# Output-weight rows loaded four to a partition, and input-weight columns read with a step of four

## The chip, the cores and the metric

The kernel runs on one core of one Trainium2 chip. The metric is the device time in microseconds (us). Of the program before there are three timed runs and one profiled execution. All kernels compute the same outputs from the same inputs.

## What is computed

A linear-attention recurrence (RWKV5) over 4 batches, 8 heads, 768 time steps and 48 channels a head feeds a two-layer perceptron with a SiLU between the layers:

```python
for t in range(S):                                   # per batch and head
    cur = outer(u * k[t], v[t])
    y[t] = r[t] @ (state + cur)
    state = w[:, None] * state + outer(k[t], v[t])
x = y as (3072 tokens, 384)
h = x @ w_in            # (384, 2048)
g = h * sigmoid(h)
out = g @ w_out         # (2048, 384)
```

All inputs and the output are 32-bit floats. Inside the kernel the perceptron's matmuls take 16-bit floats.

## The kernel before

**Units.** The 768 steps are cut into 6 chunks of 128. A unit is one chunk of one batch, so there are 24 units. Unit `i` is chunk `i // 4` of batch `i % 4`. For each unit the kernel loads r, k and v (L70), turns r and k on the tensor engine (PE, L254), applies powers of the decay (L264), forms products and sums, and evicts y in 16 bits. Then y is transposed into `xT`, the first layer's moving operand: for the first six units on PE (L465), later by a transposing transfer (L460).

**First layer.** `l1_mm` (L479) makes a piece of hidden features. `win` holds `w_in` as 128 partitions by 3 blocks `q` of 128 input features by 2048 hidden columns, in 16 bits. For hidden tile `ft` (128 of the 2048 columns, 16 tiles in all) PE loads three weight blocks, one for each `q`, and after each runs a matmul over 512 tokens (four batches) or 256 tokens (two batches, and then two tiles to a piece). `l1_silu` (L488) evicts the piece through ScalarE (ACT) into `gT`.

**Second layer.** `l2_mm` (L501) takes 128 tokens of `gT` as weights and streams `wout[:, ft, :]`, 384 columns, over the 16 tiles `ft`, four tiles to a part. `l2_last` (L525) does the same for the last unit with two column ranges.

**Weights' transfers.** `ld_win(g)` (L82) loads 512 columns of `w_in`, group `g`, and `ld_wout(g)` (L87) loads 512 rows of `w_out`, both from the queue of GpSimd (POOL), since they cast from 32 to 16 bits on the way. There are four of each.

**What sets the order.** The schedule is written by hand. Each engine runs its instructions in the order in which the program emits them. When the program is built, a wait on a semaphore is put wherever an instruction reads or overwrites a region of a tile that an earlier instruction of another engine or queue writes or reads. For the first chunk and the start of the second, the string `order` (L584) is that order, word by word; afterwards a loop over pairs of units (L617) interleaves attention steps with "fillers" from the perceptron. In the string, `L0.0` is `l1_mm` for batches 0 and 1, tiles 0 and 1; `L2.6` is batches 2 and 3, tiles 6 and 7; `L4.8` is all four batches, tile 8. A `G` word is the SiLU of the same piece. `i_q0` to `i_q3` are the four transfers of `win`, `i_o0` to `i_o3` those of `wout`. `T`, `rT`, `kT`, `kc`, `ku`, `ru`, `vu`, `S`, `Y`, `Q`, `P` are steps of a unit. `4*` in front of a word puts four matmuls of a zero tile on PE (`spin`, L163). The part that matters here reads:

```python
... 4*Y0 y160 T2 kT2 2*Y1 y161 ku2 ru2 rT2 yT0 xT0 i_q1 yT1 xT1 v162 T3 kT3 rT3 ku3 ru3 rd2
v163 4*A23 vu2 i_q2 rd3 vu3 am2 am3 L0.0 G0.0 L0.2 G0.2 Y2 y162 Y3 y163 kc0 yT2 xT2 L0.4
G0.4 kc1 yT3 xT3 L0.6 G0.6 S0 st0 kc2 T4 kT4 rT4 kc3 L2.0 G2.0 L2.2 G2.2 ku4 v164
L2.4 G2.4 S2 L2.6 G2.6 st2 ru4 i_q3 r164 L4.8 G4.8 L4.9 G4.9 rd4 ku5 kc4 kc5 sd4
L4.10 G4.10 T5 kT5 rT5 L4.11 G4.11 vu4 ru5 i_o0 v165 Q4 P4 ...
```

So three transfers of `win` are emitted ahead of `L0.0`, and the fourth between `L2.6` and `L4.8`. Hidden tiles 0 to 3 lie in group 0, tiles 4 to 7 in group 1, 8 to 11 in group 2, 12 to 15 in group 3.

Of the kernel before, what the change touches and what calls it, by code (L numbers as in the profile page):

```python
# [15 lines left out]
def kernel(  # L16
# [11 lines left out]
    nc = tc.nc  # L28
# [38 lines left out]
    win = big.tile([128, NQ, DFF], F16)  # L67
# [19 lines left out]
    def ld_wout(g):  # L87
        nc.gpsimd.dma_start(
            out=wout[:, 4 * g:4 * g + 4, :],
            in_=moe_w_out[512 * g:512 * g + 512, :].rearrange("(f p) n -> p f n", p=128))  # L90

    def columns(eng, dst, src, j):
        eng.dma_start(out=dst[64 * j:64 * j + D, :],
# [381 lines left out]
    gts = {}  # L475

    hpss = {}

    def l1_mm(sc, b0, nb, ft):  # L479
        m = B // nb  # L480
        hps = hpss[b0, ft] = ps.tile([128, m, nb * C], FP, name="hps", tag="moe", bufs=4)
        for f in range(m):
            for q in range(NQ):
                nc.tensor.matmul(hps[:, f, :], win[:, q, (ft + f) * 128:(ft + f + 1) * 128],  # L484
                                 xts[sc][:, q, b0:b0 + nb, :].rearrange("p b t -> p (b t)"),
                                 start=(q == 0), stop=(q == NQ - 1))

# [7 lines left out]
    def l1(sc, b0, nb, ft):  # L495
        l1_mm(sc, b0, nb, ft)
        l1_silu(sc, b0, nb, ft)
# [65 lines left out]
    def piece(word, f):  # L563
# [13 lines left out]
        "Y": outputs_y, "y16": evict_y, "yT": turn_y, "xT": copy_x,  # L577
        "S": first_sums, "st": first_state, "ku": bonus_ku, "ru": bonus_rku, "rd": bonus_sum,
        "r16": cast_r, "sd": decayed_state, "i_q": ld_win, "i_o": ld_wout,
        "Q": sums, "P": product_halves, "m": masked_halves, "s1_": state_first,  # L580
        "s2_": state_second, "sn": next_state, "Z": outputs_halves, "z": evict_halves,
# [14 lines left out]
    for word in order.split():  # L596
        if "*" in word:
            n, word = word.split("*")
            spin(int(n))
        if word[0] == "A":  # L600
            product_pair(int(word[1]))
        elif word in steps:
            steps[word]()
        elif word[0] == "L":
            piece(word[1:], l1_mm)
        elif word[0] == "G":
            piece(word[1:], l1_silu)
        elif word[0] == "H":
            l1(1, 0, 2, 2 * int(word[1]))
        else:  # L610
            unit_steps[word[:-1]](int(word[-1]))
# [74 lines left out]
```

## Time and profile before

| what | value |
|---|---|
| median of 3 runs (lowest to highest) | 195.09 us (194.4 to 197.38) |
| the profiled execution's own time | 194.21 us |
| its span in the profile | 192.5 us |
| PE busy | 180.4 us, 94% of the span |
| ACT, POOL, DVE (VectorE) busy | 118.5, 117.2, 107.7 us |
| first-layer matmuls (L484) | 360, the weight loads 98 ns each |
| DMA, mean over the span | 127 GB/s, about 200 GB/s in the first 45 us |
| packets of POOL's queue (q0) | 3712 packets, 3.15 MB |

The profile lists for each engine the time it was busy; "PEld" is the weight load of the tensor engine, which may run beside a matmul. A group of instructions is shown as line, engine, operation, output and input tile, shapes and count. Times in a timeline are start and length in us, counted from the start of the span; in brackets stands the idle time of the engine just before, and what ended it. A transfer's time "to landing" is counted from the start of its issue.

### The profile page before, as it was taken

To read this page: it belongs to the slowest core of one execution; us is meant where nothing else is said; L and a number is where in the kernel's file an instruction comes from. 1 tells how busy PE (TensorE), PEld (TensorE's weight loads), DVE (VectorE), ACT (ScalarE), POOL (GpSimd) and SP (SyncE) were. 2 spreads that over 40 slices of the span, in tenths; PEclk is the share of its full clock that TensorE was granted. 3 is DMA by queue.
4 is the path that set the end of the run, shared out by engine and by line. 5 is a ranking of instruction groups with operands and counts; after the bars stand their busy time and mean duration, and the time that the engine had idled before them with its cause. 6 is when DMAs were issued, how large, how long until landed. Compare 5 with 4: busy or idle time off the path is not lost. (4 is left out here: it accounts for less than half of the span.)

```text
span 192.5 us, 6544 instructions
## 1 busy us (share of the span) xinstructions
PE 180.4 (94%) x2786; PEld 112.2 (58%) x2786; DVE 107.7 (56%) x183; ACT 118.5 (62%) x235; POOL 117.2 (61%) x151
## 2 busy tenths in 40 slices
PE   7888898989999999999999999999999999899993
PEld 2455684567756876745546646557656456444562
DVE  7578775846965846836827826917924914200120
ACT  5499478779383495198593297683397773189200
POOL 6499999599899955949659459469339320000000
PEclk9999999999999999999999999999999999999999
DMA  5999999999268568278185286294286201210022
GB/s 94 215 214 198 208 200 184 159 224 217 33 117 166 184 138 169 80 149 202 29 169 136 72 178 168 46 191 125 55 166 170 41 23 66 71 52 0 2 83 83
DMA packets 90272, 24.42 MB, mean 127 GB/s; under 512 B 83329, under 2 KB 90242, under 8 KB 90242
## 3 DMA queue, kind: packets, MB, share of 16 engines
q1 hardware_dynamic: 84992, 20.39, 48.4%
q0 software_dynamic: 3712, 3.15, 10.8%
q10 hardware_dynamic: 1538, 0.46, 1.1%
q8 instruction: 22, 0.36, 0.8%
q14 instruction: 8, 0.07, 0.1%
HBM read 20.65 MB, written 4.72 MB: 132 GB/s over the span
## 5 line engine op out<-in xcount | busy, mean ns | idle before, releaser
L484 PE MATMUL hps<-xT,win 128*128 128x512 f16 (+1 forms) x360 | 66.4, 337 | 1.0 <-DMA xT<-y 0.9
L492 ACT ACTIVATE gT<-hps 128x512 f16<-128x512 f32 x96 | 55.3, 600 | 16.6 <-PE hps L484 14.1
L505 PE MATMUL ops<-wout,gT 128*128 128x384 f16 x368 | 63.0, 326 | 1.3 <-ACT gT L492 1.3
L505 PEld LDWEIGHTS <-gT 128*128 128x128 f16 x368 | 34.9, 98 | 25.4 <-ACT gT L492 2.5
L484 PEld LDWEIGHTS <-win 128*128 128x128 f16 x360 | 33.6, 98 | 26.9 <-issue 2.1
L221 POOL TENSOR_TENSOR ku<-kin,u_bc 128x384 f32<-128x384 f32 x24 | 24.7, 1029 | 15.0 <-DMA kin<-in_k_dram 11.7
L239 POOL TENSOR_TENSOR vu<-vin,rku 128x384 f32<-128x384 f32 x24 | 19.8, 837 | 19.1 <-DVE rku L234 19.1
L511 ACT COPY osb<-ops 128x384 f32<-128x384 f32 x20 | 9.6, 478 | 30.7 <-PE ops L505 27.9
L448 DVE TENSOR_TENSOR y<-yp,vu 64x384 f16<-64x384 f32 x40 | 21.3, 554 | 11.8 <-PE yp L437 5.7
L225 POOL TENSOR_TENSOR rku_f<-rin,ku 128x384 f32<-128x384 f32 x24 | 24.5, 1020 | 1.7
L392 DVE TENSOR_TENSOR s<-sp,sdec 112x384 f32<-112x384 f32 x10 | 5.6, 558 | 32.9 <-PE sp L379 30.9
L229 POOL TENSOR_TENSOR kc<-kin,lamH 128x384 f16<-128x384 f32 x20 | 20.7, 1036 | 0.0
L269 DVE TENSOR_TENSOR kT<-att,lamK 112x512 f32<-112x512 f32 x24 | 16.3, 677 | 4.7 <-PE att L261 4.7
L269 DVE TENSOR_TENSOR rT<-att,lamR 112x512 f32<-112x512 f32 x24 | 16.2, 677 | 2.3 <-PE att L261 2.3
L337 ACT CAST s1h<-s 48x384 f16<-48x384 f32 x20 | 10.2, 510 | 6.5 <-DVE s L392 6.2
L248 ACT CAST v<-vin 128x384 f16<-128x384 f32 x24 | 11.5, 510 | 2.7 <-DMA vin<-in_v_dram 2.5
L513 DVE COPY osb<-ops 128x384 f32<-128x384 f32 x3 | 1.7, 558 | 20.5 <-issue 16.4
L234 DVE TENSOR_REDUCE rku<-rku_f 128x8 f32<-128x384 f32 x24 | 12.4, 538 | 1.0 <-POOL rku_f L225 1.0
L363 DVE TENSOR_TENSOR am<-att,maskH 128x1024 f16<-128x1024 f32 x10 | 12.2, 1218 | 1.3 <-PE att L356 1.3
L283 ACT CAST rT<-rT 112x512 f16<-112x512 f32 x20 | 12.4, 620 | 0.1
L356 PE MATMUL att<-rT,kT 48*64 48x64 f32 x640 | 11.6, 220 | 0.0
L356 PEld LDWEIGHTS att<-rT,kT 48*64 48x64 f32 x640 | 10.4, 135 | 0.0
(81 smaller groups left out, 183.8 us busy)
## 6 DMA issues: line engine op xcount, KB each, us to landing
rin<-in_r_dram SPq DMA_DIRECT2D x24, 192.0 KB, 3.6
vin<-in_v_dram SPq DMA_DIRECT2D x24, 192.0 KB, 4.7
kin<-in_k_dram SPq DMA_DIRECT2D x23, 192.0 KB, 4.7
out_dram<-osb SPq DMA_DIRECT2D x23, 192.0 KB, 3.2
win<-in_moe_w_in_dram POOLq DMA_DIRECT2D x4, 384.0 KB, 6.0
wout<-in_moe_w_out_dram POOLq DMA_DIRECT2D x4, 384.0 KB, 6.4
xT<-y SPq DMA_TRANSPOSE x18, 2.3
kin<-in_k_dram ACTq DMA_DIRECT2D x1, 192.0 KB, 3.8
```

What stands on the lines that cost most here:

```text
L221: nc.gpsimd.tensor_tensor(out=L(i)["ku"], in0=kin[i % NIN][:, :, 0:D], in1=u_bc, op=ALU.mult)
L225: nc.gpsimd.tensor_tensor(out=L(i)["rku_f"], in0=rin[i % NIN][:, :, 0:D], in1=L(i)["ku"], op=ALU.mult)
L229: nc.gpsimd.tensor_tensor(out=kc[i % NIN][:, :, 0:D], in0=kin[i % NIN][:, :, 0:D], in1=lamH if unit(i)[0] else lamC, op=ALU.mult)
L234: nc.vector.tensor_reduce(out=L(i)["rku"], in_=L(i)["rku_f"], axis=mybir.AxisListType.X, op=ALU.add)
L239: nc.gpsimd.tensor_tensor(out=L(i)["vu"], in0=vin[i % NIN], in1=L(i)["rku"].unsqueeze(2).broadcast_to([128, H, D]), op=ALU.mult)
L269: nc.vector.tensor_tensor(out=L(i)[key].rearrange("p g (y t) -> p y g t", y=2), in0=L(i)["t"][0:PR, :, x], in1=lam, op=ALU.mult)
L283: nc.scalar.copy(out=L(i)["rT16"], in_=L(i)["rT"])
L356: nc.tensor.matmul(a[o0:o0 + HC, j, e, p, :], kT[r0:r0 + D, p, HC * x:HC * x + HC], rT[r0:r0 + D, p, HC * x:HC * x + HC], start=True, stop ...
L448: nc.vector.tensor_tensor(out=L(i + e)["y16"][rows].rearrange("p h d -> p (h d)"), in0=L(i)["y2"][r][rows, 0:HD], in1=L(i + e)["vu"][rows] ...
L484: nc.tensor.matmul(hps[:, f, :], win[:, q, (ft + f) * 128:(ft + f + 1) * 128], xts[sc][:, q, b0:b0 + nb, :].rearrange("p b t -> p (b t)"), ...
L492: nc.scalar.activation(out=gts[sc][:, ft:ft + m, b0 * C:(b0 + nb) * C], in_=hpss[b0, ft], func=AF.Silu)
L505: nc.tensor.matmul(opss[b], gts[sc][:, ft, b * C:(b + 1) * C], wout[:, ft, :], start=(ft == 0), stop=(ft == NFT - 1))
```

## The change

Two edits that belong together. `ld_wout` lays the 512 rows of a group out so that partition `p` holds rows `4p` to `4p + 3` of the group, instead of rows `p`, `128 + p`, `256 + p` and `384 + p`. These four rows are neighbours in memory, so a partition's part of a transfer is one run of 6144 bytes where it was four runs of 1536. The hidden feature that stands on partition `t` of tile `ft` of `wout` is now number `512 (ft // 4) + 4 t + ft % 4`. So that `gT` has the same order, the first layer's weights for tile `ft` are read from `win` as every fourth column of group `ft // 4`, from column `ft % 4` on, instead of 128 neighbouring columns. `win` is loaded as before.

```diff
     def ld_wout(g):
         nc.gpsimd.dma_start(
             out=wout[:, 4 * g:4 * g + 4, :],
-            in_=moe_w_out[512 * g:512 * g + 512, :].rearrange("(f p) n -> p f n", p=128))
+            in_=moe_w_out[512 * g:512 * g + 512, :].rearrange("(p f) n -> p f n", p=128))
...
     hpss = {}
+    win4 = win.rearrange("p q (g t c) -> p q g t c", t=128, c=4)
 
     def l1_mm(sc, b0, nb, ft):
         m = B // nb
         hps = hpss[b0, ft] = ps.tile([128, m, nb * C], FP, name="hps", tag="moe", bufs=4)
         for f in range(m):
             for q in range(NQ):
-                nc.tensor.matmul(hps[:, f, :], win[:, q, (ft + f) * 128:(ft + f + 1) * 128],
+                nc.tensor.matmul(hps[:, f, :], win4[:, q, (ft + f) // 4, :, (ft + f) % 4],
                                  xts[sc][:, q, b0:b0 + nb, :].rearrange("p b t -> p (b t)"),
                                  start=(q == 0), stop=(q == NQ - 1))
```

The order of instructions on every engine stays what it was. The waits that the build puts on them do not; on PE and POOL these differ (`<` before, `>` after; DMASW0 to DMASW3 are the four transfers of `win`, in order):

```
L0.0, 2nd weight load    < no wait                  > waits DMASW1, DMASW2
L0.4, 1st weight load    < waits DMASW1             > no wait
L4.8, 1st weight load    < waits DMASW2             > no wait
L4.8, 2nd weight load    < no wait                  > waits DMASW3
L4.12, 1st weight load   < waits DMASW3             > no wait
POOL, transfer i_q3      < no wait                  > waits PE (the last matmul of L2.6)
POOL, kc0 and kc1 (2nd)  < wait PE                  > no wait (covered by the wait above)
```

## The prediction

> **What bounds the kernel now.** The page's first part comes first: PE is busy 94% of the span. The table by stretches says where that holds.
>
> ```profile
> PE 180.4 (94%) x2786; PEld 112.2 (58%) x2786; DVE 107.7 (56%) x183; ACT 118.5 (62%) x235; POOL 117.2 (61%) x151
> ```
>
> ```profile
> 20.00:34.00 14.00, 12.21 (x222) 8.84 (x223) 9.92 (x16) 9.70 (x19) 13.88 (x16) 1.00 1.08 196
> 34.00:50.00 16.00, 14.77 (x317) 10.43 (x311) 11.30 (x19) 13.13 (x26) 13.23 (x16) 1.00 1.14 189
> 50.00:100.00 50.00, 49.92 (x827) 32.43 (x819) 32.63 (x53) 31.12 (x61) 38.52 (x45) 1.00 0.59 131
> 100.00:164.00 64.00, 62.78 (x1070) 37.67 (x1071) 36.38 (x59) 39.93 (x78) 36.27 (x41) 1.00 0.49 111
> ...
> 189.20:192.50 3.30, 0.00 (x0) 0.00 (x0) 0.00 (x0) 0.26 (x1) 0.00 (x0) 1.00 0.19 62
> ```
>
> The columns are the stretch, its length, busy time of PE, PEld, DVE, ACT, POOL, granted clock, DMA share and GB/s. PE's idle time from 20 to 164 us is 1.79 + 1.23 + 0.08 + 1.22 = 4.3 us. After 50 us PE hardly waits, so whatever PE loses early stays lost, except what those 4.3 us can give back. The chain of waits agrees: its last 25 us are PE matmuls, preceded by one transposing transfer. DMA is full up to about 48 us (share about 1), but the sorted waits from 30 to 60 us hold none of an engine for a transfer. The wout transfers, issued between 33.5 and 44 us, lie in that stretch.
>
> Then PE's timeline where the change reorders waits, and POOL's beside it:
>
> ```profile
> 19.78 1.49 PE L484 MATMUL hps<-xT,win 128*128 128x256 f16 x12
> 21.18 0.38 PE L312 MATMUL yp<-v,am 128*128 128x48 f16 x8
> 22.31 0.37 PE L312 MATMUL yp<-vx,am 128*128 128x48 f16 x8 [0.76 <-DVE am L302]
> 22.77 0.34 PE L469 MATMUL yT<-ident,y 128*128 128x128 f16 x3
> ...
> 27.92 2.77 PE L484 MATMUL hps<-xT,win 128*128 128x256 f16 x15
> ```
>
> ```profile
> 19.81 0.80 POOL L83 DMA_DIRECT2D win<-in_moe_w_in_dram  x1
> ...
> 27.28 0.80 POOL L83 DMA_DIRECT2D win<-in_moe_w_in_dram  x1
> ```
>
> The first PE row is L0.0 and L0.2, started 0.03 us before i_q2 is even issued; the last row is L2.6 (six matmuls over 256 tokens) and then L4.8 to L4.10 (nine over 512), begun after i_q3's issue. Asked for the two issues alone, the list of transfers gives 5.8 us to landing for i_q2 and 6.2 for i_q3, so they land at 25.6 and 33.5 us. Today neither is waited for.
>
> **The change part by part.**
>
> *The first new wait.* L0.0's second weight load waits for i_q2, though its columns lie in group 0. PE runs in order, so all of PE stands behind it, from about 20.0 us to 25.6. The second matmul started 0.12 us after 19.78 (12 of them take 1.49 us, the last 0.27: one in 0.11); now about 25.7. That is +5.8 us. Behind it on PE: the rest of L0.0, L0.2, Y2. ACT waits with its SiLUs, DVE with y16. POOL doesn't: its rows up to i_q3 (kc0 to kc3, ku4, ru4) need nothing of PE here.
>
> *What is given back.* Y3 waited 0.76 us for the mask product on DVE, which now is done in time; but then the transposes wait for y16 of unit 2, which DVE can only evict (0.55 us) after Y2. Replayed: Y2 ends at 27.35, y16 at 27.95, the transposes start at 28.0 against 22.77, so the shift is 5.25. The two short waits for POOL (0.21 us each, ahead of S0 and S2) go as well: 4.8 us at the end of L2.6, which now is at 28.75 (27.92, five steps of 0.11 and 0.27 for the last) and comes at 33.6.
>
> *The second new wait, a loop of two.* i_q3 now waits for L2.6's last matmul, and L4.8's second weight load waits for i_q3. L4.8 is the very next step on PE. Issue at about 33.65 instead of 27.28; landing 5.8 to 6.2 us later (its own rows; I take 6.0, the median of the four), at 39.65; the matmul starts at 39.8 instead of 28.8 (27.92, six matmuls of 0.11 and one of 0.22 us before it). The shift is 11.0 us. Queued behind i_q3 on POOL are ku5, kc4, kc5, the decayed state, vu4, ru5, i_o0: they come 6.4 us later, PE 11, so PE finds them done. SP's own transfers reuse buffers that POOL frees, by the same 6.4, less than PE's shift. The last wout transfer comes behind vu5, which waits for DVE and so for PE: it moves as PE does, and its landing (at 50.2, the part that needs it not before 52.5) keeps its place.
>
> *After that.* PE's waits for POOL go (0.42 us at 31.96), the one for ACT's cast of v (0.94) stays, since ACT casts behind the SiLU of L4.11. I take 0.6 given back: +10.4 us.
>
> *The clock.* Twice PE now stands still, 5.6 and 6.1 us. The longest idle stretch in the trace is the 3.3 us after the last matmul, at a granted clock still 1.00; so from below the cost is nothing. From above: the spins at the start.
>
> ```profile
> 2.97 1.91 PE L166 MATMUL zs<-idle 128*128 128x512 f16 x4
> ...
> 6.31 1.04 PE L166 MATMUL zs<-idle 128*128 128x512 f16 x4
> ```
>
> Four equal matmuls take 1.91 us at first and 1.04 later. The slow pace lasts from 1.29 to about 5.5 us, 4.2 us, in which work for 4.2 x 1.04/1.91 = 2.3 us gets done: 1.9 us lost. At most that after each stall, 3.8; I take half, 1.9, as the trace decides neither way. The Trainium skill, TensorE: Matmul & The Clock Gate, Part 1, speaks against the change here: it says that the array falls to half clock after one idle window of about 3.4 us and needs a busy one to come back. No row before has an idle stretch that long; by that rule, an estimate, each stall costs half of such a window, 1.7 us, and the sum would be 208.
>
> *Strided weight loads.* 360 loads read every fourth column. Each has a matmul to hide under: 109 ns (256 tokens; by the loops 144 of them) or 216 ns (512 tokens; 216 of them). Recorded are 98 ns today, and their pace where nothing hides them is
>
> ```profile
> 21.17 0.27 PEld L312 LDWEIGHTS <-am 128*128 128x128 f16 x8 [0.19 <-DVE am L302]
> ```
>
> that is (270 - 98)/7 = 25 ns. From below: nothing, a hidden load can't give time. From above: four times that pace, 100 ns, and the 37 ns by which a load of 32-bit columns (L356, 135 ns) is longer than one of 16-bit; 137 ns would show 28 ns on 144 matmuls, 4 us, and about 0.1 us on each of some 40 first loads behind a wait, 4 us: 8 us. I take 0, the 25 ns being nearer than any row with a step. The skill's TensorE: Matmul & The Clock Gate, Weight-path perf modes, lets the fast load take strided columns, and its section LDWEIGHTS gives P/1.2, 107 ns for 128 columns, without it; by either it stays hidden, and the sum is the same.
>
> *The wout transfers.* 2048 runs become 512 if each goes as one packet: q0 falls from 3712 to 2176. Issue costs 0.80 us for 384 runs (win) and 0.80 for 512 (wout), so POOL saves nothing. No wait of the trace ends with wout; between -0.5 and +0.5 us for traffic beside it, I take 0.
>
> *Sum.* 5.8 - 1.0 + 6.2 (33.65 + 6.0 + 0.15 - 28.8 - 4.8) - 0.6 = 10.4, and 1.9 for the clock: 12.3 on the profiled execution's 194.21 (span 192.5, 1.7 around it) gives 206.5. That execution is 0.9 under the median, 195.09, so the forecast is 11.4 over the median.
>
> **The rivals.**
>
> *Strides show.* The same two stalls and the 8 us: 214.5. Against it: the spare 11 to 118 ns under every matmul. It would show as matmuls of L484 spaced wider than 109 and 216 ns.
>
> *A quick i_q3.* Issued 6 us later, it may meet emptier queues: a transfer of half its size lands in a median 3.6 us. Then the second stall is 2.4 us shorter and the second clock loss falls away: 203.1. Against it: DMA moves 189 GB/s from 34 to 50 us too, as SP's transfers fill the queues.
>
> *The loss is given back (not slower).* One mechanism, PE's own slack: with other engines ahead, PE's waits vanish. Its whole idle time is 192.5 - 180.4 = 12.1 us; if all of it absorbed the two waits (12.0 without what is already given back) the time is 194 to 195. It decides from 8.1 us given back on (12.0 less 2% of 195, 3.9). Only 4.3 us lie between 20 and 164 us, so at best 194.2 + 12.0 - 4.3 = 202.
>
> *The transfers matter (faster).* DMA bounds the first 48 us and fewer packets shorten it. q0 takes 10.8% of 16 engines' span, half of it wout's; but PE's waits that end with a transfer are 0.7 + 0.9 us in all: 193 at best, and the new waits must not bind.
>
> **How the numbers follow.** Two stalls as replayed 0.68, at 206.5; strides as well 0.14, up to 214.5; a quick i_q3 0.12, at 203; given back 0.04; faster 0.02. A measurement of this kernel can tell about 2% from no change, 3.9 us. Slower by over 2%: 0.68 + 0.14 + 0.12 = 0.94; within: 0.04; faster: 0.02. The range goes from 201.5 (a quick i_q3 and no clock loss, less the rest of the slack) to 213 (3.8 us of clock, half of the strides' bound and more): it leaves out the two last cases and the upper end of the strides.
>
> **What would show it.** Right: PE idle about 5.6 us after one L484 matmul near 20 us, ended by a win transfer; i_q3 issued near 33.6, about 0.1 us after L2.6; PE idle about 6 us again, ended by it; from 50 us on the same rows 10 to 12 us later; in the granted clock a dip behind one or both stalls. L484's spacing still 109 and 216 ns. Wrong: PE at L0.2 before 25 us, a stall below 4 us, or a shift at 50 us that differs by more than 3 us from that at L4.8.

## The result, and the profile after

The changed kernel took 210.04 us (208.65 to 211.08, four runs) against 195.94 for the kernel before beside it: a ratio of 1.0743, with a 95% interval of 1.062 to 1.0867. (The ratio compares the means of the fast runs, which leave out one run of the kernel before, at 197.38 us; its median has that run.) It is slower. The profiled execution took 210.78 us, with a span of 209.1, 16.6 more than before. From the page of the changed kernel, busy times, the two rows of PE by slices and of its granted clock, POOL's DMA queue, and the first layer's groups:

```profile
PE 185.9 (89%) x2786; PEld 119.2 (57%) x2786; DVE 108.2 (52%) x183; ACT 119.0 (57%) x235; POOL 116.4 (56%) x151
...
PE   7898079078899999999999999999999999989993
...
PEclk9999859959999999999999999999999999999999
...
q0 software_dynamic: 2176, 3.15, 9.7%
...
L485 PE MATMUL hps<-xT,win 128*128 128x512 f16 (+1 forms) x360 | 69.9, 348 | 12.7 <-DMA win<-in_moe_w_in_dram 11.8
...
L485 PEld LDWEIGHTS <-win 128*128 128x128 f16 x360 | 39.1, 115 | 36.4 <-issue 9.3
```

The first-layer matmuls, whose line is now 485, waited 11.8 us for transfers of win. All of that is in two holes of PE's row, slices 5 and 8 of 40 (5.2 us each), and the clock's row dips in and behind the first (slices 5 and 6) and behind the second (slice 9). POOL's queue fell to the 2176 packets that four rows to a packet give. The timeline of PE, and below it that of POOL:

```profile
6.94 1.89 PE L166 MATMUL zs<-idle 128*128 128x512 f16 x4
...
21.05 0.30 PE L485 MATMUL hps<-xT,win 128*128 128x256 f16 x1
26.82 2.51 PE L485 MATMUL hps<-xT,win 128*128 128x256 f16 x11 [5.47 <-DMA win<-in_moe_w_in_dram]
...
35.77 1.06 PE L485 MATMUL hps<-xT,win 128*128 128x256 f16 x7
43.16 3.60 PE L485 MATMUL hps<-xT,win 128*128 128x512 f16 x8 [6.33 <-DMA win<-in_moe_w_in_dram]
...
51.05 1.49 PE L485 MATMUL hps<-xT,win 128*128 128x512 f16 x6
...
184.78 10.52 PE L485 MATMUL hps<-xT,win 128*128 128x512 f16 x48 [0.87 <-DMA xT<-y]
```

```profile
21.08 0.80 POOL L83 DMA_DIRECT2D win<-in_moe_w_in_dram  x1
...
36.91 0.80 POOL L83 DMA_DIRECT2D win<-in_moe_w_in_dram  x1 [8.35 <-PE hps L485]
...
43.11 0.61 POOL L88 DMA_DIRECT2D wout<-in_moe_w_out_dram  x1
```

One matmul of L0.0 runs; the next comes 5.8 us later, when i_q2 has landed. Six of L2.6 and one of L4.8 run; POOL, idle for 8.35 us, may now issue i_q3; 6.2 us later it has landed, and PE goes on. That is the loop: PE holds POOL, then POOL's transfer holds PE.

The shift against the kernel before, at six places of PE's timelines, says where the 16.6 us came in. Two rows of the kernel before that it rests on:

```profile
34.43 1.47 PE L484 MATMUL hps<-xT,win 128*128 128x512 f16 x6
...
168.19 10.52 PE L484 MATMUL hps<-xT,win 128*128 128x512 f16 x48 [0.87 <-DMA xT<-y]
```

| place | before | after | shift | added here |
|---|---|---|---|---|
| first matmul of L0.0 | 19.78 | 21.05 | 1.27 | 1.27 |
| its second | 19.90 | 26.82 | 6.92 | 5.65 |
| first of L2.6 | 27.92 | 35.77 | 7.85 | 0.93 |
| second of L4.8 | 28.80 | 43.16 | 14.36 | 6.51 |
| first of L4.12 | 34.43 | 51.05 | 16.62 | 2.26 |
| first of the last L484/L485 run | 168.19 | 184.78 | 16.59 | -0.03 |

After 50 us nothing is added and nothing given back. The 1.27 us at the top are no part of the change, as neither a wait nor a read differs up to there: in this execution the tensor engine ran its first matmuls at half pace for longer (the spins at 6.94 us took 1.89 us, where in the execution before the four at 6.31 took 1.04). The kernel with the step alone, below, has the same waits and starts L0.0 at 19.79. The 2.26 us are the clock, and the 0.93 the clock less some 0.6 that PE gets back; the kernel with spins, below, parts the two. The table by stretches of 2 us has it in the last column but two:

```profile
22.00:24.00 2.00, 0.00 (x0) 0.00 (x0) 1.52 (x2) 0.00 (x0) 2.00 (x3) 1.00 1.27 231
24.00:26.00 2.00, 0.00 (x0) 0.00 (x0) 0.00 (x0) 0.00 (x0) 2.00 (x3) 0.52 1.22 199
26.00:28.00 2.00, 1.18 (x6) 0.88 (x7) 0.00 (x0) 0.00 (x0) 1.92 (x3) 0.50 0.97 197
28.00:30.00 2.00, 1.97 (x23) 1.44 (x20) 0.24 (x1) 1.19 (x2) 0.57 (x1) 0.50 1.04 204
30.00:32.00 2.00, 1.63 (x16) 1.55 (x17) 0.78 (x2) 0.84 (x2) 0.00 (x0) 0.78 1.06 211
...
40.00:42.00 2.00, 0.00 (x0) 0.00 (x0) 0.00 (x0) 0.00 (x0) 2.00 (x3) 0.78 1.07 172
42.00:44.00 2.00, 0.84 (x2) 0.29 (x3) 0.00 (x0) 0.00 (x0) 1.71 (x3) 0.50 0.10 16
44.00:46.00 2.00, 2.00 (x6) 0.73 (x5) 0.00 (x0) 1.08 (x2) 0.00 (x0) 0.50 0.79 121
46.00:48.00 2.00, 2.00 (x19) 1.05 (x18) 0.16 (x1) 0.71 (x2) 0.00 (x0) 0.51 0.39 75
48.00:50.00 2.00, 1.06 (x39) 0.51 (x38) 1.13 (x2) 1.28 (x3) 0.00 (x0) 1.00 0.00 0
```

A stretch at 0.52 was at half clock for 1.92 of its 2 us, one at 0.78 for 0.88. So the clock was halved from 24.1 to 30.9 and from 41.1 to 48.0 us, 6.8 us each. Of these PE had work from 26.8 and 43.2 on: 4.1 and 4.8 us at half pace, worth 2.0 and 2.4 us. It falls once more behind the last matmul, which ends at 205.74 us:

```profile
206.00:209.10 3.10, 0.00 (x0) 0.00 (x0) 0.00 (x0) 0.04 (x1) 0.00 (x0) 0.88 0.21 66
```

### The profile page after: what moved, and what is told of

Its sections match the earlier page's. It is cut to its first block, busy times and chain, and to the rows that moved or that the text cites. A ratio compares the mean times of both kernels' runs of the same rounds, so it can differ in the third digit from the quotient of the medians.

```text
span 209.1 us, 6545 instructions
## 1 busy us (share of the span) xinstructions
PE 185.9 (89%) x2786; PEld 119.2 (57%) x2786; DVE 108.2 (52%) x183; ACT 119.0 (57%) x235; POOL 116.4 (56%) x151
## 3 DMA queue, kind: packets, MB, share of 16 engines
q0 software_dynamic: 2176, 3.15, 9.7%
## 5 line engine op out<-in xcount | busy, mean ns | idle before, releaser
L485 PE MATMUL hps<-xT,win 128*128 128x512 f16 (+1 forms) x360 | 69.9, 348 | 12.7 <-DMA win<-in_moe_w_in_dram 11.8
L485 PEld LDWEIGHTS <-win 128*128 128x128 f16 x360 | 39.1, 115 | 36.4 <-issue 9.3
L239 POOL TENSOR_TENSOR vu<-vin,rku 128x384 f32<-128x384 f32 x24 | 19.8, 838 | 28.8 <-DVE rku L234 28.8
L221 POOL TENSOR_TENSOR ku<-kin,u_bc 128x384 f32<-128x384 f32 x24 | 24.7, 1029 | 14.4 <-DMA kin<-in_k_dram 10.8
L448 DVE TENSOR_TENSOR y<-yp,vu 64x384 f16<-64x384 f32 x40 | 21.3, 553 | 11.8 <-PE yp L437 5.7
L261 PE MATMUL att<-ident,kin 64*112 64x64 f32 x192 | 10.1, 228 | 0.8 <-DMA kin<-in_k_dram 0.8
```

What stands on the lines that cost most here:

```text
L221: nc.gpsimd.tensor_tensor(out=L(i)["ku"], in0=kin[i % NIN][:, :, 0:D], in1=u_bc, op=ALU.mult)
L239: nc.gpsimd.tensor_tensor(out=L(i)["vu"], in0=vin[i % NIN], in1=L(i)["rku"].unsqueeze(2).broadcast_to([128, H, D]), op=ALU.mult)
L448: nc.vector.tensor_tensor(out=L(i + e)["y16"][rows].rearrange("p h d -> p (h d)"), in0=L(i)["y2"][r][rows, 0:HD], in1=L(i + e)["vu"][rows] ...
L485: nc.tensor.matmul(hps[:, f, :], win4[:, q, (ft + f) // 4, :, (ft + f) % 4], xts[sc][:, q, b0:b0 + nb, :].rearrange("p b t -> p (b t)"), s ...
```

## The experiments

The theory: the build's new waits make the loss, through two stalls of PE and the clock behind each. Rival A: reading weights with a step of four is slow. Rival B: the larger packets do harm. In the ratios below, each kernel is set against the kernel before that ran beside it.

**The packets alone.**

```diff
-                nc.tensor.matmul(hps[:, f, :], win4[:, q, (ft + f) // 4, :, (ft + f) % 4],
+                nc.tensor.matmul(hps[:, f, :], win[:, q, (ft + f) * 128:(ft + f + 1) * 128],
```

> One half of the change alone: wout in runs of four rows, the first layer's weights read as before in 128 neighbouring columns (the hidden features then don't match wout's rows; work and shapes are the same). No wait differs from before. Theory (the new waits of PE and of i_q3 do the harm): as before, 195 us; the wout transfers land sooner than 6.4 us, and q0 has 2176 packets. Rival A (reading with a step of four is slow): 195 too. Rival B (the larger packets do the harm, by what they hold up on the 16 engines): about 210.

In this kernel and the next one the hidden features don't match the rows of `wout`, so their outputs are not those of the other kernels; the work and the shapes are the same.

Measured: 194.53 us, ratio 0.9983 (0.9935 to 1.0031). Rival B falls. The packets did what they are for: from this kernel's page,

```profile
q0 software_dynamic: 2176, 3.15, 9.7%
...
wout<-in_moe_w_out_dram POOLq DMA_DIRECT2D x4, 384.0 KB, 5.1
```

a wout transfer lands in a median 5.1 us (4.7 to 6.7) instead of 6.4 (6.1 to 6.7), by the four transfers of one execution each (5.9 in the kernel with four tiles below). Nobody waited for it, so this brings nothing. The 4.7 us of the changed kernel are not the packets' merit alone: its transfers run later, beside less traffic, and there the old packets, in the next kernel, land in 4.9 us.

**The step alone.**

```diff
-            in_=moe_w_out[512 * g:512 * g + 512, :].rearrange("(p f) n -> p f n", p=128))
+            in_=moe_w_out[512 * g:512 * g + 512, :].rearrange("(f p) n -> p f n", p=128))
```

> The other half alone: columns with a step of four, wout loaded as before (again features and rows don't match; same work). All the new waits are there. Theory: 210 us, with PE idle 5.5 us after one matmul near 21 us, 6.3 us near 37 us, and half clock behind each. Rival A: 210. Rival B: 195.

Measured: 210.4 us, ratio 1.0765 (1.0687 to 1.0843): the whole loss, with both stalls (5.76 and 5.92 us by PE's timeline). It lies in this half, by the waits or by the step itself.

**The whole change without the waits: four tiles.**

```diff
-    win = big.tile([128, NQ, DFF], F16)
+    win = [big.tile([128, NQ, 512], F16, name=f"win{g}") for g in range(4)]
...
-            out=win[:, :, 512 * g:512 * g + 512],
+            out=win[g],
...
-    win4 = win.rearrange("p q (g t c) -> p q g t c", t=128, c=4)
+    win4 = [t.rearrange("p q (t c) -> p q t c", c=4) for t in win]
...
-                nc.tensor.matmul(hps[:, f, :], win4[:, q, (ft + f) // 4, :, (ft + f) % 4],
+                nc.tensor.matmul(hps[:, f, :], win4[(ft + f) // 4][:, q, :, (ft + f) % 4],
```

> The whole change, but each column group of win is a tile of its own, so a read of one group can't wait for the transfer of another; PE then waits for the four transfers at the places where it did before. Every strided load and every large packet stays. Theory: 195 us, within 2, no idle stretch of PE above 1 us between 20 and 50 us. Rival A: 210, as all 360 loads keep the step. Rival B: 210.

Measured: 194.48 us, ratio 0.9973 (0.9939 to 1.0007), which can't be told from no change. Its table by stretches has PE as busy as before the change (there 12.21 and 14.77 us), and its list on win gives the weight loads and matmuls (lowest, median, highest ns):

```profile
20.00:34.00 14.00, 12.21 (x209) 9.50 (x213) 9.83 (x16) 9.51 (x19) 13.88 (x16) 1.00 1.09 197
34.00:50.00 16.00, 14.94 (x330) 11.37 (x325) 11.94 (x19) 13.22 (x26) 12.45 (x16) 1.00 0.98 188
```

```profile
L485 PEld LDWEIGHTS <-win x360: 110/113/135, 19.9 to 178.3; 128*128 128x128 f16 x180
L485 PE MATMUL hps<-xT,win x360: 269/379/408, 19.9 to 178.5; 128*128 128x512 f16 x108, 128*128 128x256 f16 x72
```

A load with the step takes 113 ns instead of 98, and next to all of it is hidden: L0.0 and L0.2 together take 1.50 us, with 1.49 before. Rival A falls, the theory stands: every strided load and every packet of the change is here, and the loss is not.

**What makes the waits: win by column group first.**

```diff
-    win = big.tile([128, NQ, DFF], F16)
+    win = big.tile([128, 4, NQ, 512], F16)
...
-            out=win[:, :, 512 * g:512 * g + 512],
+            out=win[:, g],
...
-    win4 = win.rearrange("p q (g t c) -> p q g t c", t=128, c=4)
+    win4 = win.rearrange("p g q (t c) -> p g q t c", c=4)
...
-                nc.tensor.matmul(hps[:, f, :], win4[:, q, (ft + f) // 4, :, (ft + f) % 4],
+                nc.tensor.matmul(hps[:, f, :], win4[:, (ft + f) // 4, q, :, (ft + f) % 4],
```

> The whole change, with win one tile but laid out by column group first, then by the block of 128 input features, so that a transfer's part of a partition is one unbroken range (3 x 512 columns) where it was three pieces 2048 columns apart. Theory (a read of every fourth column is tested against the whole stretch from a transfer's first to its last column, in which the other groups' columns lie): no read lies in another transfer's stretch, the waits stand where they stood before the change, 195 us. Rival (any read with a step waits for every transfer of its tile): 210.

Measured: 194.64 us, ratio 1.0015 (0.9974 to 1.0055). The built program's waits stand where they stood before the change, with one tile and with every read strided, and PE's timeline has no wait for win:

```profile
19.82 1.50 PE L485 MATMUL hps<-xT,win 128*128 128x256 f16 x12
...
27.97 2.79 PE L485 MATMUL hps<-xT,win 128*128 128x256 f16 x15
```

So it is not the step by itself. It agrees with the place of the changed kernel's new waits too: they stand at second weight loads, which read block `q` = 1, where the columns lie between another transfer's first and last column; the loads of `q` = 0 just ahead of them got none. That the build compares such whole stretches when a read has a step is inferred from these waits, not seen in its workings.

**One wait at a time: groups 0 and 1, then groups 2 and 3.** Both kernels lay out two groups in the new way and two in the old (the other kernel has `g >= 2` and `ft >= 8`).

```diff
-            in_=moe_w_out[512 * g:512 * g + 512, :].rearrange("(p f) n -> p f n", p=128))
+            in_=moe_w_out[512 * g:512 * g + 512, :].rearrange(
+                "(p f) n -> p f n" if g < 2 else "(f p) n -> p f n", p=128))
...
+    def columns_of(q, ft):
+        if ft < 8:
+            return win4[:, q, ft // 4, :, ft % 4]
+        return win[:, q, ft * 128:(ft + 1) * 128]
...
-                nc.tensor.matmul(hps[:, f, :], win4[:, q, (ft + f) // 4, :, (ft + f) % 4],
+                nc.tensor.matmul(hps[:, f, :], columns_of(q, ft + f),
```

> The change for column groups 0 and 1 alone (tiles 0 to 7), the old layout for groups 2 and 3. L0.0 still waits for i_q2 and i_q3 for L2.6, but L4.8 no longer waits for i_q3; only L4.12 does, as before. Theory: the first stall and its clock loss, and at most a short wait at L4.12, since i_q3 lands near 42 us and L4.12 is due near 41: 5.0 + 2.0 + 1, so 202 to 204 us. Rival A (half of the strided loads): 202.5 as well, but then spread over the span, with no idle stretch.

> The change for column groups 2 and 3 alone (tiles 8 to 15). L0.0 waits as before, and i_q3 waits for nothing; L4.8's second weight load waits for i_q3. Theory: one stall at L4.8, from about 29 us to i_q3's landing near 33.5: 4.7 us, perhaps without a clock loss as it is shorter than both of the others; less 0.6 given back: 198 to 200. Rival (half of the strided loads): 202.5, without a stall.

Measured for groups 0 and 1: 201.63 us, ratio 1.0331 (1.0257 to 1.0404), just below the 202 to 204. PE's timeline:

```profile
20.08 0.30 PE L491 MATMUL hps<-xT,win 128*128 128x256 f16 x1
26.65 2.51 PE L491 MATMUL hps<-xT,win 128*128 128x256 f16 x11 [6.27 <-DMA win<-in_moe_w_in_dram]
...
42.38 1.47 PE L491 MATMUL hps<-xT,win 128*128 128x512 f16 x6 [0.41 <-DMA win<-in_moe_w_in_dram]
```

i_q3 is as late as in the changed kernel, but with the work of L4.8 to L4.11 and of the next unit ahead of the wait, 0.41 us of the second stall is left. Measured for groups 2 and 3: also 201.63, ratio 1.0352 (1.0313 to 1.0391), above the 198 to 200. PE's timeline, and a table by stretches:

```profile
27.94 1.04 PE L491 MATMUL hps<-xT,win 128*128 128x256 f16 x7
33.91 3.60 PE L491 MATMUL hps<-xT,win 128*128 128x512 f16 x8 [4.92 <-DMA win<-in_moe_w_in_dram]
```

```profile
28.00:34.00 6.00, 1.08 (x10) 0.65 (x9) 2.13 (x4) 1.63 (x4) 5.98 (x8) 0.88 1.13 200
34.00:38.50 4.50, 4.50 (x25) 1.86 (x26) 0.00 (x0) 1.79 (x3) 0.30 (x1) 0.50 0.94 135
38.50:50.00 11.50, 9.66 (x200) 6.15 (x199) 7.98 (x13) 7.64 (x15) 5.75 (x7) 0.96 0.75 132
```

The stall is 4.92 us, about the 4.7 foreseen. The miss is the clock: it was thought perhaps safe at this length, but by these stretches it was halved from about 32.6 to 39.4 us, through the first 5.5 us of the work that followed. Both kernels stall and neither is slower in an even way, as rival A would have it.

**The clock apart from the waits: spins in front of them.**

```diff
-        v163 4*A23 vu2 i_q2 rd3 vu3 am2 am3 L0.0 G0.0 L0.2 G0.2 Y2 y162 Y3 y163 kc0 yT2 xT2 L0.4
+        v163 4*A23 vu2 i_q2 rd3 vu3 am2 am3 24*L0.0 G0.0 L0.2 G0.2 Y2 y162 Y3 y163 kc0 yT2 xT2 L0.4
...
-        L2.4 G2.4 S2 L2.6 G2.6 st2 ru4 i_q3 r164 L4.8 G4.8 L4.9 G4.9 rd4 ku5 kc4 kc5 sd4
+        L2.4 G2.4 S2 L2.6 G2.6 st2 ru4 i_q3 r164 27*L4.8 G4.8 L4.9 G4.9 rd4 ku5 kc4 kc5 sd4
```

> The changed kernel with its two waits as they are, and matmuls of a zero tile put on PE in front of them: 24 ahead of L0.0 and 27 ahead of L4.8, 5.2 and 5.8 us at 216 ns. PE then works where it stood still; i_q3's issue isn't later, since it waits for L2.6, ahead of the second lot. Theory (of the 15 us, some 4.4 are the lost clock behind the stalls): the waits cost what they did, the clock stays, 205 to 206 us. If the clock costs nothing by itself: 210. If the spins' zero tile doesn't keep the clock: 210, with the dips still in the granted clock.

Measured: 207.66 us, ratio 1.0663 (1.0613 to 1.0713). The clock's row of its page has a 9 in all 40 slices. PE's timeline:

```profile
25.11 0.27 PE L485 MATMUL hps<-xT,win 128*128 128x256 f16 x1
26.37 1.37 PE L485 MATMUL hps<-xT,win 128*128 128x256 f16 x11 [0.99 <-DMA win<-in_moe_w_in_dram]
...
28.66 0.34 PE L469 MATMUL yT<-ident,y 128*128 128x128 f16 x3 [0.52 <-DVE y L317]
...
33.82 0.84 PE L485 MATMUL hps<-xT,win 128*128 128x256 f16 x6
...
40.33 0.38 PE L485 MATMUL hps<-xT,win 128*128 128x512 f16 x1
41.97 1.92 PE L485 MATMUL hps<-xT,win 128*128 128x512 f16 x8 [1.27 <-DMA win<-in_moe_w_in_dram]
...
47.66 1.49 PE L485 MATMUL hps<-xT,win 128*128 128x512 f16 x6
```

Eleven matmuls take 1.37 us here and 2.51 in the changed kernel, eight longer ones 1.92 and 3.60: the half clock, undone by work that computes nothing. The saving is 2.4 us by the medians, not the 4 to 5 expected. From the second matmul of L0.0 to the first of L2.6 it is 7.45 us against 8.95, and from L4.8's second to L4.12's first (47.66) 5.69 against 7.89: 3.7 us saved. But both transfers landed later, 6.3 and 7.0 us after their issue instead of 5.6 and 6.2, which takes 1.5 back. Why they did is open.

**The loop apart from the first wait: i_q3 early.**

```diff
-        v163 4*A23 vu2 i_q2 rd3 vu3 ...
+        v163 4*A23 vu2 i_q2 i_q3 rd3 vu3 ...
...
-        L2.4 G2.4 S2 L2.6 G2.6 st2 ru4 i_q3 r164 ...
+        L2.4 G2.4 S2 L2.6 G2.6 st2 ru4 r164 ...
```

> The changed kernel with i_q3 issued right behind i_q2, ahead of L0.0. L0.0's second weight load then waits for i_q3 as well, and the loop of i_q3 and L4.8 is gone. Theory: one longer stall, to i_q3's landing near 28 to 29 us, 7 to 8 us, with one clock loss of 2, about 203. Rival (a stall is a stall, the shift is set by when the last of win lands and not by the loop): the same as the changed kernel without its second stall's 6.3 us, but 2 to 3 us more in the first: 206.

Measured: 204.18 us, ratio 1.0498 (1.0464 to 1.0533). PE's timeline:

```profile
20.19 0.30 PE L485 MATMUL hps<-xT,win 128*128 128x256 f16 x1
28.79 2.51 PE L485 MATMUL hps<-xT,win 128*128 128x256 f16 x11 [8.30 <-DMA win<-in_moe_w_in_dram]
...
37.51 2.79 PE L485 MATMUL hps<-xT,win 128*128 128x256 f16 x15
```

One stall of 8.3 us, to 28.8 as foreseen, and L4.8 follows L2.6 without a gap (15 matmuls in one row). The time lies between the 203 and the rival's 206. Without the second stall (6.33 us) but with the longer first one (8.30 for 5.47) the changed kernel's 210.04 becomes 206.5, which is the rival's number; less the 2.2 us of clock behind the second stall it is 204.3, close to the 204.18 measured. So the loop cost a second stall and a second clock loss, less the 2.8 us by which the one stall is longer: about 6 us of the changed kernel's 14 to 15.

This execution also shows that the clock falls without a stall. From its page and PE's timeline:

```profile
PEclk9969958999999999999999999999999999999999
```

```profile
6.10 1.04 PE L166 MATMUL zs<-idle 128*128 128x512 f16 x4
...
11.88 1.89 PE L166 MATMUL zs<-idle 128*128 128x512 f16 x4
```

The 6 in the third slice is half clock from about 11.0 to 14.4 us, where PE had not been idle for more than 0.75 us at a time since its first matmul. The kernels with the packets alone and with four tiles dip there too, at an overall clock of 0.989. It costs little: L0.0 starts 0.41 us later here than in the kernel before (20.19 and 19.78), and 0.14 us later with four tiles. What brings it about is open.

None of the versions in these experiments is faster than the kernel before: the two that take the waits out agree with it within 0.7%.

## Why the prediction was right

It was right in direction and mechanism, and 3.5 us low in size: 206.5 us forecast, 210.04 measured, inside 201.5 to 213. Against the profiled execution (210.78) it is 4.3 us low: 1.8 from the clock, 1.1 from what it thought would be given back, 0.2 from the two waits, and 1.27 from that execution's start. By its own steps:

- *The first wait*, +5.8: +5.65. The place, the transfer and the landing (5.6 us after the issue, taken as 5.8) were right.
- *Given back before L2.6*, -1.0, and *after L4.8*, -0.6: where the clock held, in the kernel with spins, L2.6's first matmul comes 5.9 us late behind a shift of 6.47: -0.57. From L4.8 to L4.12 nothing is given back there (13.17 and 13.23 us late). So 0.5 instead of 1.6. What came back is the 0.55 that was replayed up to the transposes, which start 5.89 us late (28.66 and 22.77). The waits for POOL, 0.42 us ahead of S0 and S2 and 0.42 at 31.96, gave nothing: they are idle time of the weight loads (PEld), and PE's own rows before the change have no idle stretch there (one row starts at 31.21 us and takes 0.82, the next starts at 31.96). The wait for ACT's cast, 0.94 us, stayed, as foreseen.
- *The loop*, +6.2: +6.51, with 6.2 us from issue to landing, where 6.0 was taken.
- *The clock*, the mis-sized term: 1.9 for both stalls, as half of what the start of the kernel bounded; against the kernel with spins it was 1.5 and 2.2, 3.7 in all. (At half pace for 4.1 and 4.8 us it would be 2.0 and 2.4; some of that ran beside waits that were there anyway.) Neither stall kept its clock, so half was the wrong choice between the bounds; and the upper bound, 1.9 for each, was itself a little low for the second. It was read from 4.2 us of slow matmuls at the start of one execution; in the next one the slow pace still held at 6.94 us. The lower bound, nothing, was read from a clock of 1.00 in the 3.3 us behind the last matmul, which don't bear it: in the changed kernel's execution the clock falls in that stretch (0.88), and in the two stalls it fell 2.7 and 4.3 us after PE's last matmul (21.35 to 24.1, 36.83 to 41.1). Nor does a full reading say much at the start: the clock's row has a 9 in its second slice, where the spins at 6.94 us ran at half pace.
- The Trainium skill's rule that the prediction set beside that term (TensorE: Matmul & The Clock Gate, Part 1) was the better guide: no idle stretch of 4.9 us or longer in these runs kept its clock, and its estimate, 1.7 us for each stall, is near the 1.5 and 2.2. That the estimate came so near is partly luck. The clock was down for 6.8 us at each stall and not for one window of 3.4, and the loss depends on how much of that falls on work. It also fell as early as 2.5 us into a stall (groups 0 and 1), and in three executions with no stall, so 3.4 us of idle time is not a length up to which these runs were safe.
- *Strided loads*, 0: 0, with 113 ns instead of 98, hidden. The same page's Weight-path perf modes, by which the fast load takes columns with a step, fits that; these runs don't prove it, as a load without the fast mode would have stayed hidden too by the prediction's own reckoning. Its rival, at 214.5, is refuted by the two kernels that keep the step without the waits.
- *wout's transfers*, 0: 0 for the time. That POOL saves nothing was wrong: the issue took 0.60 us and not 0.80, which no one waits for.
- *A quick i_q3* did not happen (6.2 us), nor was the loss given back: PE's shift was the same at 51 and at 185 us.

The terms as measured, 5.65 + 6.51 + 3.7 - 0.5 = 15.4, and the 1.27 us of this execution's start make the 16.6 of the span. Since the clock's part and what was given back were taken from the same rows and the kernel with spins, that sum is bound to close; what supports the split is that kernel, where the clock held.

## What to carry to other kernels

A change of an access pattern can change waits without moving any instruction: list the waits of the built program before and after, and price each new one by what is issued behind it. Where two such waits close a loop, an engine ahead of a queue and the queue ahead of the same engine, the latency of the transfer is paid in full, however early the data could have come. A tile laid out so that each transfer fills one unbroken range, or a tile for each transfer, keeps them away at no cost that these runs could tell (194.48 and 194.64 us).

## What the runs showed of the hardware

- PE's clock was halved in every stall of 4.92 us or more (4.92, 5.47, 5.76, 5.92, 6.27, 6.33, 8.30), between 2.5 and 4.4 us after PE's last matmul, and stayed halved for 6.8 us each time, part of it on the work behind the stall. Behind the kernel's last matmul it fell within 3.3 us in the changed kernel and not in the kernel before. In three executions it was also halved for 3.4 us near 11 to 14.4 us, where PE had not been idle for 1 us at a time since its first matmul; why is open. In the kernel with groups 2 and 3 a stall of 4.92 us made the time 6.7 us longer (201.63 against 194.9).
- Weight loads of 128 columns at a step of 8 bytes are recorded with 113 ns, at neighbouring columns with 98. Under a matmul of 109 ns spacing the difference hardly shows (1.50 against 1.49 us for twelve).
- POOL's issue of a casting transfer took 0.80 us for 384 or 512 runs (0.93 for the first one of each execution) and 0.60 for 128.
